# Border by halves, first expert in sequence, last routing in fine steps, no whole float32 weights

## Chip, cores and metric

The kernel runs on one core of one Trainium2 chip. The metric is device microseconds from one launch. A core has a matrix engine (TensorE, PE in the profile; PEld are its weight loads), a vector engine (VectorE, DVE), a scalar engine (ScalarE, ACT), GpSimd (POOL) and SyncE (SP), which here only issues transfers. Each engine works through its own queue in order, and waits at an instruction until what it needs is there. Transfers are issued from SP, ACT and POOL.

## What is computed

Retention attention over two batches (768 steps, 8 heads of 64), then two mixture-of-experts layers (MoE) over the 1536 tokens of width 512, each with 8 experts of inner width 1024. The first skips tokens whose skip score is not positive and adds its result to x; the second places at most a capacity of tokens per expert, in order.

```python
for t in range(S):
    state = gamma * state + k[:, :, t] (outer) v[:, :, t]
    y[:, :, t] = scale * q[:, :, t] @ state
...
do_compute = x @ w_skip > 0                      # first MoE
e_idx = argmax(xc @ w_gate); gate_w = softmax at e_idx
out[do_compute] = xc + gate_w * (relu(xc @ w1[e]) @ w2[e])
...
e = argmax(x @ w_gate2)                          # second MoE
keep token i if fewer than capacity tokens before it chose e
out[i] = gate_w[i] * (relu(x[i] @ w1[e]) @ w2[e])
```

## The kernel before

**Attention.** The 768 steps are cut into six chunks c of 128, and units (c, b) run over chunks and batches. `scores` (L592) forms q k products, which DVE multiplies by a decay mask into p (L607); `state` adds k v products into u (L620), for which POOL scales k with `scale_k` (L575, the tile is called big, since k and v lie in a raw buffer of that name) and q with `scale_q` (L591); `outs` forms the result xt (L637, L644). Beside it a generator `sink` routes the chunk before: logits (L375), their sums (L385), a choice by DVE (mx, d, rm, t, tm, m, then the gate's se, sf and a reciprocal), transposed rows rowc (L394), ranks (L313 ff.), slots (pr, sl, where) and `to_slots` (L327), which adds token numbers into a slot table tab. The rows of a chunk are written to a table in memory by `write_rows` (L339). Between steps, `pump` moves weights one piece on.

**Weights.** Chunks of 1 MB (w1a, w2a of MoE 1, w1b, w2b of MoE 2; two halves j per expert) are loaded by SP into five raw buffers, all called big (L210). A chunk is then divided into two float32r parts, hi by ACT (L237) and lo by DVE (L240, raw minus hi): in the attention in pieces of 128x512, later of 128x1024, so that a chunk is two pieces of each. A product with divided operands is three matmuls (`mm3`, L759 to L761: hi hi, lo hi, hi lo). Four of MoE 1's chunks (w2a of the odd experts, j = 1) are not divided but used as whole float32 (L789), with a whole transposed hTw. In the attention, pump divides on two of three turns from chunk 1 on.

**Border.** `last_chunk` (L461) routes the last chunk one batch after the other and gathers expert 0's rows from the chunks before into a0 (issued in `sink`, L346); `place` (L356) adds the last chunk's rows through a one-hot oh, then a0 through the identity, and `split` (L362, L363) makes xh on ACT and xl on DVE, by which layer 1 of expert 0 begins.

**Experts.** For expert e, `layer1` gives h (24 matmuls of 128x512, called s in the rows), h is transposed into hT (L738) and split into hTh and hTl, the next expert's rows are transposed into x, and `layer2` (24 matmuls, called o) runs one expert behind. Its result goes to `route_b` (L806), a generator stepped beside the main line: DVE makes row (L810, x plus gated result), TensorE transposes it (L824), forms the second MoE's logits (L830, L835), DVE chooses (mx to reciprocal), then ranks and slots (prb, slb, whereb), and `to_slots`. The order of every engine's queue is the order in which this code issues. `step_side` advances the generators and pump.

**Second MoE.** After the last routing, blocks (0,0) and (0,1) of expert 0 (128 rows each) run singly, then experts 1 to 7 in pairs of blocks (256 columns). The rows of a block are gathered by ids_b. `emit_out` (L860) scales a result on ACT into y and scatters it from POOL.

Of the kernel before, what the change touches and what calls it, by code (L numbers as in the profile page):

```python
# [41 lines left out]
def kernel(  # L42
# [53 lines left out]
    def load_first():  # L96

        qk, kv = qk_tile(a_p), take_kv()
        for b in range(B):
            nc.sync.dma_start(out=qk[:, :, b], in_=qkv[0, :, 0:2, b])  # L100
            nc.sync.dma_start(out=kv[:, 1, b], in_=qkv[0, :, 3, b])
        nc.sync.dma_start(out=kv[:, 0], in_=qkv[0, :, 2])
        return qk, kv
# [101 lines left out]
    def load_w():  # L205
        while count["load"] < len(order) and len(raw_free) > kept[0] and raw_free[0][0] <= count["turn"]:
# [4 lines left out]
            key, _, divided = order[i]  # L211
            if divided:
                raw_t[i] = (t, count["turn"])
            else:
                wt[key], held[key] = t.rearrange("p (k f) -> p k f", k=4), t

    def next_split():

        while count["split"] < len(order) and not order[count["split"]][2]:
            count["split"] += 1  # L220
# [24 lines left out]
    def used(key):  # L245
        pool = held.pop(key)
        if key in whole_keys:
            raw_free.append((0, pool))
        else:
            w_free.append((count["turn"] + 2, pool))  # L250

    whole_keys = {o[0] for o in order if not o[2]}
# [29 lines left out]
    def pick(lg, nt, ng, rm, gate_out):  # L282
# [10 lines left out]
        ex = sm.tile([128, n, 8], F32, tag=f"ex{n}", name="ex")  # L293
        nc.scalar.activation(out=ex, in_=d, func=ACTF.Exp)
        t = t9[n]
        nc.vector.scalar_tensor_tensor(out=t[:, :, 0:8], in0=d, scalar=0.0, in1=rm, op0=ALU.is_equal, op1=ALU.mult)
        tm = sm.tile([128, n, 1], F32, tag=f"tm{n}", name="tm")
# [4 lines left out]
        def gate():  # L302
            se = sm.tile([128, nt, ng, 1], F32, tag=f"se{n}", name="se")
            nc.vector.tensor_reduce(out=se, in_=ex.rearrange("p (a g) j -> p a g j", a=nt), axis=AX.X, op=ALU.add)  # L304
            sf = sm.tile([128, nt, ng], F32, tag=f"sf{n}", name="sf")
            nc.vector.tensor_scalar(out=sf, in0=se.rearrange("p a g o -> p a (g o)"), scalar1=1e-9, scalar2=None, op0=ALU.add)
            nc.vector.reciprocal(out=gate_out, in_=sf)
# [925 lines left out]
```

## Time and profile before

| | us |
|---|---|
| median of three runs (414.24 to 416.0) | 414.49 |
| the profiled execution | 413.43 |
| its span in the trace | 411.6 |
| TensorE busy | 381.8 |
| DVE busy | 247.3 |
| ACT busy | 210.0 |
| POOL busy | 119.4 |

The profiled execution took 1.8 us more than its span, and 1.06 less than the median. Times inside the trace count from the span's start. In rows of a timeline the bracket behind an operation gives the idle time of its engine just before it, and what ended it. "x4" merges four like instructions; their time runs from the first's start to the last's end, and since matmuls overlap, distances are best read from one start to the next.

### The profile page before, as it was taken

To read this page: it belongs to the slowest core of one execution; us is meant where nothing else is said; L and a number is where in the kernel's file an instruction comes from. 1 tells how busy PE (TensorE), PEld (TensorE's weight loads), DVE (VectorE), ACT (ScalarE), POOL (GpSimd) and SP (SyncE) were. 2 spreads that over 40 slices of the span, in tenths; PEclk is the share of its full clock that TensorE was granted. 3 is DMA by queue.
4 is the path that set the end of the run, shared out by engine and by line. 5 is a ranking of instruction groups with operands and counts; after the bars stand their busy time and mean duration, and the time that the engine had idled before them with its cause. 6 is when DMAs were issued, how large, how long until landed. Compare 5 with 4: busy or idle time off the path is not lost.

```text
span 411.6 us, 6872 instructions
## 1 busy us (share of the span) xinstructions
PE 381.8 (93%) x2665; PEld 311.9 (76%) x2665; DVE 247.3 (60%) x440; ACT 210.0 (51%) x318; POOL 119.4 (29%) x184
## 2 busy tenths in 40 slices
PE   8879999688999999999886999999999999999993
PEld 4768778566767667766554899898989889898982
DVE  4646776549896896896652497274555637364310
ACT  1435553258776677667431665374535556354301
POOL 3665764271044043033034210311304030130202
PEclk8998999989999999999999999999999999999998
DMA  8997965749988887987963287475865657520101
GB/s 292 418 419 279 352 245 148 304 117 352 388 298 335 325 304 285 344 273 287 344 233 91 83 265 262 161 258 204 271 217 182 216 184 231 191 76 2 50 3 39
DMA packets 18336, 95.99 MB, mean 233 GB/s; under 512 B 2481, under 2 KB 2737, under 8 KB 8824
## 3 DMA queue, kind: packets, MB, share of 16 engines
q1 hardware_dynamic: 12068, 80.33, 53.6%
q0 software_dynamic: 3280, 9.76, 7.3%
q10 hardware_dynamic: 2948, 5.39, 3.5%
q8 instruction: 23, 0.38, 0.4%
q14 instruction: 17, 0.14, 0.1%
HBM read 87.03 MB, written 9.48 MB: 234 GB/s over the span
## 4 chain that ended last, share of the span: by engine, by line
PE 66%; DVE 12%; DMA 10%; ACT 6%; issue 5%; POOL 1%; SPq 0%; POOLq 0%; DVEq 0%; ACTq 0%
PE s L759 10%; PE s L761 10%; PE s L760 10%; PE o L761 7%; PE o L759 7%; PE o L760 7%; DVE lo L240 5%; DMA big<-in_w1a_dram 4%; ACT hi L237 4%; PE o L789 2%; DMA table<-rowc 2%; DVE xl L363 2%; PE m L644 2%; DMA wgt<-in_wg_dram 2%; PE m L637 1%
## 5 line engine op out<-in xcount | busy, mean ns | idle before, releaser
L240 DVE TENSOR_TENSOR lo<-big,hi 128x1024 fp32r<-128x1024 f32 (+1 forms) x126 | 145.1, 1184 | 56.0 <-ACT hi L237 55.4
L237 ACT ACTIVATE hi<-big 128x1024 fp32r<-128x1024 f32 (+1 forms) x126 | 121.8, 1014 | 3.5 <-DMA big<-in_w1a_dram 3.5
L759 PE MATMUL o<-hi,hTh 128*128 128x512 f32 x176 | 72.1, 409 | 0.3 <-ACT hTh L362 0.3
L761 PE MATMUL o<-hi,hTl 128*128 128x512 f32 x176 | 70.0, 398 | 1.0 <-DVE hTl L363 1.0
L760 PE MATMUL o<-lo,hTh 128*128 128x512 f32 x176 | 69.7, 396 | 0.0
L761 PE MATMUL s<-xh,lo 128*128 128x256 f32 x224 | 63.4, 283 | 0.0
L760 PE MATMUL s<-xl,hi 128*128 128x256 f32 x224 | 63.4, 283 | 0.0
L759 PE MATMUL s<-xh,hi 128*128 128x256 f32 x224 | 63.4, 283 | 0.0
L865 POOL DMA_INDIRECT out_dram<-y,ixo x16 | 18.2, 1137 | 142.2 <-ACT y L862 121.8
L759 PEld LDWEIGHTS s<-xh,hi 128*128 128x128 f32 x224 | 43.0, 192 | 0.3
L760 PEld LDWEIGHTS s<-xl,hi 128*128 128x128 f32 x224 | 43.0, 192 | 0.3
L761 PEld LDWEIGHTS s<-xh,lo 128*128 128x128 f32 x224 | 43.0, 192 | 0.0
L761 PEld LDWEIGHTS o<-hi,hTl 128*128 128x128 f32 x176 | 33.1, 188 | 9.7 <-DVE hTl L363 1.8
L759 PEld LDWEIGHTS o<-hi,hTh 128*128 128x128 f32 x176 | 33.1, 188 | 7.1 <-ACT hTh L362 0.5
L760 PEld LDWEIGHTS o<-lo,hTh 128*128 128x128 f32 x176 | 33.3, 189 | 6.7
L996 DVE SCALAR_TENSOR_TENSOR hTl<-s,hTh 128x512 fp32r<-128x512 f32 x28 | 19.3, 688 | 31.7 <-ACT hTh L995 31.7
L759 PE MATMUL s<-hi,xh 128*128 128x512 f32 x80 | 35.5, 444 | 2.2 <-ACT xh L362 1.3
L995 ACT ACTIVATE hTh<-s 128x512 fp32r<-128x512 f32 x28 | 16.7, 598 | 40.2 <-PE s L761 40.2
L862 ACT ACTIVATE y<-o,rowc 128x512 f32<-128x512 f32 x15 | 10.3, 689 | 47.2 <-issue 29.4
L761 PE MATMUL s<-hi,xl 128*128 128x512 f32 x80 | 32.1, 401 | 0.8 <-DVE xl L363 0.8
L760 PE MATMUL s<-lo,xh 128*128 128x512 f32 x80 | 31.9, 399 | 0.0
L842 POOL TENSOR_SCALAR rhsb<-m,cs 128x8 bf16<-128x8 bf16 x8 | 2.5, 306 | 85.2 <-DVE se L304 73.3
(151 smaller groups left out, 545.2 us busy)
## 6 DMA issues: line engine op xcount, KB each, us to landing
big<-in_w1a_dram SPq DMA_DIRECT2D x16, 1024.0 KB, 6.6
big<-in_w2a_dram SPq DMA_DIRECT2D x16, 1024.0 KB, 6.8
big<-in_w1b_dram SPq DMA_DIRECT2D x16, 1024.0 KB, 5.4
big<-in_w2b_dram SPq DMA_DIRECT2D x16, 1024.0 KB, 5.0
qk<-in_qkv_dram SPq DMA_DIRECT2D x5, 1024.0 KB, 9.8
big<-in_qkv_dram SPq DMA_DIRECT2D x5, 1024.0 KB, 6.4
table<-rowc ACTq DMA_DIRECT2D x5, 516.0 KB, 7.7
table<-row ACTq DMA_DIRECT2D x8, 258.0 KB, 4.0
```

The source lines that it names most:

```text
L237: nc.scalar.activation(out=hi[:, k], in_=r3[:, k], func=ACTF.Copy)
L240: nc.vector.tensor_tensor(out=lo[:, k], in0=r3[:, k], in1=hi[:, k].bitcast(F32), op=ALU.subtract)
L363: nc.vector.tensor_tensor(out=lo, in0=src, in1=hi.bitcast(F32), op=ALU.subtract)
L644: nc.tensor.matmul(out=o[64 * j:64 * j + 64, 128 * r:128 * r + 128], lhsT=v[:, b, 2 * r + j, :], rhs=pt[c, b][j][:, r, :], start=not c and ...
L759: nc.tensor.matmul(out=acc, lhsT=a[0], rhs=w[0], start=first, stop=False)
L760: nc.tensor.matmul(out=acc, lhsT=a[0], rhs=w[1], start=False, stop=False)
L761: nc.tensor.matmul(out=acc, lhsT=a[1], rhs=w[0], start=False, stop=last)
L789: nc.tensor.matmul(out=acc, lhsT=a[0][:, k % 4, :], rhs=w[:, k % 4, :], start=k == 0, stop=k == FT - 1)
L862: nc.scalar.activation(out=y, in_=acc, func=ACTF.Copy, scale=xs[:, GCOL + 1:GCOL + 2])
L865: new = nc.gpsimd.indirect_dma_start(out=out[:, :], out_offset=bass.IndirectOffsetOnAxis(ap=ix, axis=0), in_=y, in_offset=None, bounds_che ...
L995: nc.scalar.activation(out=hi[:, g:g + 2, :], in_=acc, func=ACTF.Relu)
L996: nc.vector.scalar_tensor_tensor(out=lo[:, g:g + 2, :], in0=acc, scalar=0.0, in1=hi[:, g:g + 2, :].bitcast(F32), op0=ALU.max, op1=ALU.subtract
```

## The change

It does seven things. (1) The first loads: v of both batches comes in one transfer instead of two, after the qk of both. (2) No weight is used whole: all of w2a is divided. (3) The order of weights has w2a of expert 0 ahead of w1a of expert 1, and the main line runs layer 2 of expert 0 directly after its layer 1; from expert 1 on layer 2 is again one behind. (4) In the attention pump divides on three of four turns from chunk 2 on; `scale_k` and the decays are issued earlier. (5) The rows of a chunk are written before the ranks are formed; the last chunk's rows go out in one transfer from SP; the border places and splits by halves, and slot sums, ids and gathers of the last chunk (`gather_all`) are issued after the first six matmuls of expert 0. (6) `mm3s` takes two k at a time, four matmuls with hi and then two with lo; x of the next expert is turned after the first six matmuls of layer 2, and `to_slots` of an expert comes one step later. (7) The last routing is stepped between matmuls of layer 1 of block (0,0), in fine steps; x of block (0,1) is transposed after all of layer 2, and the last y is scaled half on ACT and half on DVE.

```diff
-        nc.sync.dma_start(out=kv[:, 0], in_=qkv[0, :, 2])
+        for i in (1, 0):
+            nc.sync.dma_start(out=kv[:, i], in_=qkv[0, :, 2 + i])
...
-            order.append(((kind, e, j), ap[e, j], not whole(kind, e, j)))
-
-    def whole(kind, e, j):
-
-        return kind == "w2a" and e % 2 == 1 and j == 1
+            order.append(((kind, e, j), ap[e, j]))
...
-        if e:
-            add_chunks(w2a, e - 1, "w2a")
+        if e != 1:
+            add_chunks(w2a, e - 1 if e else 0, "w2a")
...
             rows_T(xt, rc, 1, psum)
+            write_rows(nc.scalar, rc, B)
             yield
...
             where = [slots_of(sl, i) for i in bs]
-            write_rows(nc.scalar, rc, B)
...
             place(acc, *late[0], True, False)
-            where = [slots_of(sl[b], 0) for b in range(B)]
-            for b in range(B):
-                gates[b]()
-                write_rows(nc.scalar, rc[:, b:b + 1, :], 1)
-            place(acc, *late[1], False, False)
-            for b in range(B):
-                to_slots(where[b], rhs[b][:, 0], 0, 16)
-            nc.vector.tensor_copy(out=ids, in_=tab)
...
+            gate(ex, B, 2, rc[:, :, GCOL:GCOL + 2])
+            write_rows(nc.sync, rc, B)
             for g in range(2):
                 ks = slice(2 * g, 2 * g + 2)
+                place(acc, *late[1], False, False, range(KT)[ks])
                 place(acc, a0, ident, False, True, range(KT)[ks])
...
+            def gather_all():
+                where = [slots_of(sl[b], 0, sm, "whereb", 2) for b in range(B)]
+                for b in range(B):
+                    to_slots(where[b], rhs[b][:, 0], 0, 16)
+                nc.vector.tensor_copy(out=ids, in_=tab)
+                for e in (1, 0, 2, 3):
+                    xs1[e] = gather(ids[:, e:e + 1], 1 + NT)
...
-                pump(4, count["turn"] % 3 > 0)
+                pump(4, c >= 2 and count["turn"] % 4 > 0)
...
+            if b == 0 and 0 < c < NCH - 1:
+                scale_k(c)
             yield
...
-                if c + 1 < NCH - 1:
-                    scale_k(c + 1)
...
+    def mm3s(acc, pairs, first, last):
+
+        todo = [(a[0], w[i]) for a, w in pairs for i in range(2)] + [(a[1], w[0]) for a, w in pairs]
+        for i, (a, w) in enumerate(todo):
+            nc.tensor.matmul(out=acc, lhsT=a, rhs=w, start=first and i == 0, stop=last and i == len(todo) - 1)
+            if i % 2 and i < len(todo) - 1:
+                yield
...
-        yield from idle(2 if e < E - 1 else 1)
+        yield from idle(3 if e < E - 1 else 1)
         to_slots(where, rhs, 8, 8)
...
+    h0 = []
+    first = layer1(x, "w1a", 0, h0)
+    next(first)
+    x0[1]()
+    step_side()
+    h = run(first)
+    xs1[4] = gather(ids[:, 4:5], 1 + NT)
+    second = layer2(h0, "w2a", 0)
...
+        if e > 1:
+            second = layer2(hT.pop(e - 1), "w2a", e - 1)
+            next(second)
+            step_side()
+            x = turned(xs1[e + 1] if e + 1 < E else a0, 0, "x")
...
+            acc = run(second)
+            then_route(e - 1, acc, *((2, 1) if e < E - 1 else (0, 0)))
...
+    last = route_b(E - 1, xs1[E - 1], acc, 0, 0)
+    next(last)
+    pieces[0] = 0
...
+    first = layer1(x, "w1b", 0, h0, True)
+    for i in range(1, 13):
+        next(first)
+        if i % 3 == 0:
+            step_side()
+        if i in (2, 4, 5, 9, 12):
+            next(last)
```

The first place is DVE's queue at the end of chunk 1's routing in the attention, where the first weight split stands (where are the slots, lo the split, p the masked scores, mx to m the choice for the next chunk). Before:

```order
L420 TENSOR_SCALAR where<-iota,sl 128x257 x2
L240 TENSOR_TENSOR lo<-big_88,hi 128x512
L607 TENSOR_TENSOR p<-s,mask 128x512 x2
L240 TENSOR_TENSOR lo<-big_88,hi 128x512
L607 TENSOR_TENSOR p<-s,mask 128x512 x2
L287 TENSOR_REDUCE mx<-s 128x4
```

After, from the same slots on:

```order
L412 TENSOR_SCALAR where<-iota,sl 128x257 x2
L605 TENSOR_TENSOR p<-s,mask 128x512 x4
L272 TENSOR_REDUCE mx<-s 128x4
L275 TENSOR_TENSOR d<-s,mx 128x32
L261 SCALAR_TENSOR_TENSOR rm<-s,cs 128x2x8 x2
```

Two pieces of lo that stood ahead of the two pairs of p have gone behind the choice.

The second place is SP's queue around the border, from the last k and v load on (big from in_w1a or in_w2a are weight chunks, table is the write of the last chunk's rows). Before, where that write is on ACT's queue:

```order
L82 DMA big_89<-in_qkv_dram 128x2048
L210 DMA big_85<-in_w2a_dram 128x2048
L210 DMA big_88<-in_w2a_dram 128x2048
L210 DMA big_86<-in_w1a_dram 128x2048
L210 DMA big_89<-in_w1a_dram 128x2048
L210 DMA big_87<-in_w2a_dram 128x2048
```

After:

```order
L82 DMA big_88<-in_qkv_dram 128x2048
L206 DMA big_85<-in_w2a_dram 128x2048
L206 DMA big_89<-in_w1a_dram 128x2048
L206 DMA big_86<-in_w1a_dram 128x2048
L328 DMA table<-rowc_108 128x2x516
L206 DMA big_87<-in_w1a_dram 128x2048
L206 DMA big_88<-in_w1a_dram 128x2048
```

The two loads of expert 2's w1a now stand behind the table write of the last chunk; before, they followed the loads ahead of them without a write between.

The third place is DVE's queue in the last routing, around the row of expert 7 (row with the second number; the first line closes the gate of expert 6, or follows it). Before:

```order
L307 RECIPROCAL row_1188<-sf 128x1
L240 TENSOR_TENSOR lo<-big_88,hi 128x1024 x2
L810 SCALAR_TENSOR_TENSOR row_1189<-o,rowc_107 128x512
L848 TENSOR_TENSOR prb<-t,m 128x8
L850 TENSOR_REDUCE slb<-prb 128x1
L852 TENSOR_SCALAR whereb<-iota,slb 128x257
L287 TENSOR_REDUCE mx<-t 128x1
```

After:

```order
L298 RECIPROCAL row_1153<-sf 128x1
L230 TENSOR_TENSOR lo<-big_86,hi 128x1024
L850 TENSOR_TENSOR prb<-t,m 128x8
L852 TENSOR_REDUCE slb<-prb 128x1
L854 TENSOR_SCALAR whereb<-iota,slb 128x257
L230 TENSOR_TENSOR lo<-big_86,hi 128x1024
L811 SCALAR_TENSOR_TENSOR row_1154<-o,rowc_106 128x512
L272 TENSOR_REDUCE mx<-t 128x1
```

The slots of expert 6 (prb, slb, whereb), which wait for its ranks, now stand ahead of expert 7's row, between the two lo pieces.

## Rows read from the trace of the kernel before

**Rows 1.** Stretches: PE, PEld, DVE, ACT, POOL busy, granted PE clock, DMA share, GB/s.

```profile
32.00:35.40 3.40, 3.40 (x41) 3.28 (x38) 2.66 (x13) 2.37 (x7) 1.78 (x3) 0.51 1.01 419
222.00:226.00 4.00, 1.40 (x9) 1.14 (x9) 0.00 (x0) 0.59 (x1) 3.08 (x4) 1.00 0.54 148
120.00:210.00 90.00, 85.22 (x447) 60.16 (x447) 70.33 (x125) 56.60 (x84) 22.43 (x37) 1.00 0.84 305
226.00:390.00 164.00, 164.00 (x1051) 147.85 (x1050) 91.43 (x106) 85.42 (x113) 32.20 (x41) 1.00 0.52 179
```

**Rows 2.** Whom PE waits for, whole span: us in total, times, longest.

```profile
PE t L738 <- DMA rowc<-table,ids_b: 2.6, 1, 2.6
...
PE s L375 <- DVE p L607: 2.0, 1, 2.0
PE t L824 <- DVE row L810: 1.9, 2, 1.5
...
PE u L620 <- POOL big L575: 1.3, 2, 1.0
...
PE t L738 <- ACT h L779: 1.1, 1, 1.1
PE o L761 <- DVE hTl L363: 1.0, 1, 1.0
```

**Rows 3.** Timeline, DVE then ACT, before 30: start, us, operation, idle before it.

```profile
28.38 0.89 DVE L240 TENSOR_TENSOR lo<-big,hi 128x512 fp32r<-128x512 f32 x1 [4.50 <-ACT hi L237]
...
27.72 1.15 ACT L237 ACTIVATE hi<-big 128x512 fp32r<-128x512 f32 x2 [3.23 <-DMA big<-in_w1a_dram]
```

**Rows 4.** The chain that ended last, at the border: start, us, what.

```profile
69.35 6.62 DMA table<-rowc
...
76.83 4.47 DMA a<-table,ids
...
83.43 0.79 PE s L759
```

**Rows 5.** Transfers issued at 56 to 68, then 69.2 to 80: KB, us to landing.

```profile
table<-rowc ACTq DMA_DIRECT2D x1, 516.0 KB, 4.3
...
big<-in_w1a_dram SPq DMA_DIRECT2D x2, 1024.0 KB, 6.0
```

**Rows 6.** Timeline of DVE at the border and in the experts of MoE 1.

```profile
82.51 0.87 DVE L363 TENSOR_TENSOR xl<-m,xh 128x256 fp32r<-128x256 f32 x2 [2.77 <-ACT xh L362]
...
89.55 2.36 DVE L240 TENSOR_TENSOR lo<-big,hi 128x1024 fp32r<-128x1024 f32 x2 [4.36 <-ACT hi L237]
...
127.98 0.17 DVE L287 TENSOR_REDUCE mx<-t 128x1 f32<-128x8 f32 x1 [3.08 <-PE t L835]
...
142.97 0.17 DVE L287 TENSOR_REDUCE mx<-t 128x1 f32<-128x8 f32 x1 [1.37 <-PE t L835]
...
153.00 0.74 DVE L810 SCALAR_TENSOR_TENSOR row<-o,rowc 128x512 f32<-128x512 f32 x1
...
158.05 0.17 DVE L287 TENSOR_REDUCE mx<-t 128x1 f32<-128x8 f32 x1 [3.11 <-PE t L835]
...
188.09 0.17 DVE L287 TENSOR_REDUCE mx<-t 128x1 f32<-128x8 f32 x1 [3.09 <-PE t L835]
```

**Rows 7.** Timeline of PE around one expert of MoE 1.

```profile
147.66 1.88 PE L789 MATMUL o<-big,hTw 128*128 128x512 f32 x4
149.74 0.26 PE L327 MATMUL tab<-rhsb,whereb 128*128 128x8 bf16 x4 [0.20 <-DVE whereb L852]
...
152.45 0.48 PE L759 MATMUL s<-hi,xh 128*128 128x512 f32 x1
...
153.93 0.60 PE L824 MATMUL t<-cs,row 128*128 128x128 f32 x4
```

**Rows 8.** Timeline of PE, the first matmul of block (0,1).

```profile
226.69 0.47 PE L759 MATMUL s<-hi,xh 128*128 128x512 f32 x1
```

**Rows 9.** Timeline of ACT, the last result.

```profile
404.77 0.69 ACT L862 ACTIVATE y<-o,rowc 128x512 f32<-128x512 f32 x1 [2.12 <-PE o L761]
```

More of the change, by code (lines that the diff above doesn't have):

```diff
@@ L210, in load_w @@
             nc.sync.dma_start(out=t, in_=order[i][1])
[L211 to L215, printed above, removed]
+            raw_t[i] = (t, count["turn"])
     def next_split():
-        while count["split"] < len(order) and not order[count["split"]][2]:
-            count["split"] += 1
         i = count["split"]
@@ L245, in used @@
     def used(key):
[L246 to L252, printed above, removed]
+        w_free.append((count["turn"] + 2, held.pop(key)))
     splitting = []
@@ L677, in main @@
                 yield from scores(c, 1)
+                if c and c + 1 < NCH:
+                    decays(c + 1)
                 if c == 0 and pump:
@@ L784, in layer2 @@
         acc = psum("o", 2)
-        for k in range(FT):
+        for k in range(0, FT, 2):
             w = wt[kind, e, k // 4]
             a = hT[k // 4]
-            if whole(kind, e, k // 4):
-                nc.tensor.matmul(out=acc, lhsT=a[0][:, k % 4, :], rhs=w[:, k % 4, :], start=k == 0, stop=k == FT - 1)
-            else:
-                mm3(acc, at_k(a, k % 4), at_k(w, k % 4), k == 0, k == FT - 1)
-            if k % 4 == 3 and done_with(kind, e):
+            ks = (k % 4, k % 4 + 1)
+            for _ in mm3s(acc, [(at_k(a, i), at_k(w, i)) for i in ks], k == 0, k == FT - 2):
+                pass
+            if k % 4 == 2 and done_with(kind, e):
                 used((kind, e, k // 4))
-            if k % 2 == 1:
-                yield
+            yield
         return acc
@@ L919, in then_route @@
         return g
-    for e in range(E):
-        h = run(layer1(x, "w1a", e))
+    h0 = []
[7 more added lines that the diff above has]
+    next(second)
+    h0.append(turned(h, 1, "hT"))
+    step_side()
+    next(second)
+    step_side()
+    x = turned(xs1[1], 0, "x")
+    acc = run(second)
+    then_route(0, acc, 1, 1)
+    for e in range(1, E):
+        first = layer1(x, "w1a", e)
+        if e == 1:
+            for _ in range(2):
+                next(first)
+                step_side()
+            x = turned(xs1[2], 0, "x")
+        h = run(first)
         if e + 4 < E:
@@ L941, in load_block @@
         xs2[e, j] = gather(ids_b[:, 8 * j + e:8 * j + e + 1])
-    def after_routing():
-        while last in side:
-            yield
-        nc.vector.tensor_copy(out=ids_b, in_=tab[:, 8:24])
-        for e, j in ((0, 1), (1, 0), (1, 1), (2, 0), (2, 1)):
-            load_block(e, j)
-        yield
-    side.append(after_routing())
-    h0 = []
-    h = run(layer1(x, "w1b", 0, h0))
+    h0 = []
+    first = layer1(x, "w1b", 0, h0, True)
+    for i in range(1, 13):
+        next(first)
+        if i % 3 == 0:
+            step_side()
+        if i in (2, 4, 5, 9, 12):
+            next(last)
+    try:
+        next(first)
+    except StopIteration as stop:
+        h = stop.value
+    nc.vector.tensor_copy(out=ids_b, in_=tab[:, 8:24])
+    for e, j in ((0, 1), (1, 0), (1, 1), (2, 0), (2, 1)):
+        load_block(e, j)
+    second = layer2(h0, "w2b", 0)
+    next(second)
     h0.append(turned(h, 1, "hT"))
-    second = layer2(h0, "w2b", 0)
-    for _ in range(FT // 2 - 1):
-        next(second)
-        step_side()
+    acc = run(second)
     while side:
@@ L961 @@
     x = turned(xs2[0, 1], 0, "x")
-    acc = run(second)
+    pieces[0] = 1
     ct = totals([cum[:, 0, :], cumb])
@@ L1021 @@
     h = run(layer1(x, "w1b", 0, h0))
+    second = layer2(h0, "w2b", 0)
+    next(second)
+    h0.append(turned(h, 1, "hT"))
+    step_side()
     x = pair_T(1)
-    h0.append(turned(h, 1, "hT"))
     flag = overflow(ct)
-    acc = run(layer2(h0, "w2b", 0))
+    acc = run(second)
     emit_out(xs2[0, 1], acc)
```

163 lines of the change are left out of this document (87 added, 76 removed).

## Prediction, made before the change was run

> **What bounds the kernel now.** I read the table of stretches first [rows 1]. From 226 to 390, which is the pair loop of the second MoE, TensorE works in all 164.00 of 164 us: nothing there can be gained by an order. From 120 to 210, the experts of the first MoE, it works 85.22 of 90, and the rest of its idle time lies in the attention, at the border between attention and MoE, and at the last routing. So the second view is who TensorE waits for [rows 2]: 1.3 us for POOL's scaled k, 2.0 for the product with the mask (p), 2.6 for a gather, 1.9 for row, 1.1 for h, 1.0 for hTl. Behind each I looked at the releaser's engine. The p that came late stood on DVE behind a weight split lo, which had waited 4.50 us for ACT's hi, which had waited 3.23 us for a weight load from memory [rows 3]. At the border the chain is a write of the table (6.62 us), then the gather that reads it (4.47 us), and the first expert matmul starts at 83.43 [rows 4].
>
> In the experts I ask which engine sets the period. Per expert DVE runs from mx (142.97) through six lo pieces, an xl and the slot sums to row (153.00): 10.03 us, and row takes 0.74 [rows 6]. TensorE transposes that row (153.93), and 4.12 us later the next mx can start (158.05) [rows 6, 7]. A closed loop DVE to TensorE to DVE of 10.03 + 0.74 + 0.05 + 4.12 = 14.9 us. From mx at 127.98 to mx at 188.09 there are four periods of 15.03 [rows 6]. So DVE's queue is nearly the bound already, though it works fewer of the 90 us than TensorE does.
>
> **The attention: -5.0 us.** Splits now begin with chunk 2, not 1, so the first lo is queued behind the where and p of chunk 1 and finds its weights landed: the 2.0 (1.97) goes. POOL scales k before the gate work and the decays: the 1.3 goes. Behind the late p the clock fell to half: 0.51 granted over 3.4 us, so 3.4 x 0.49 = 1.7 us [rows 1]. If the idle goes, I count that too. Sum 5.0. The same twelve split pieces lie in later turns, between masks and gate work that leave DVE gaps, and the earlier scaling only changes the order on POOL, before operations that wait for TensorE anyway. Bounds: 3.3 if the half-clock stretch comes anyway, 5.3 if the start's two combined v loads also hide the 0.3 us wait for qk.
>
> **The border: -2.2 us.** An equal write of 516 KB with nothing beside it landed in 4.3 us; this one took 6.62 because two 1 MB loads were issued with it [rows 5]. In the new order no weight load stands on SP between expert 1's first-layer chunks and the last chunk's table write, so chunk 4's write should land at about 73.5 and its gather at 78 to 79 instead of 81.3. TensorE gets there at about 77.5. By halves (two transposes, a 128x256 split of 0.43, then matmuls) I work out the first expert matmul at 81.2 instead of 83.43. The slot sums leave this path and stand behind the first six matmuls. Bounds: 0 if the write is no faster, 2.7 if the gather hides wholly. The last chunk's write goes from two on ACT to one on SP, where the next loads queue behind it; they have six chunks of work ahead of them.
>
> The Trainium skill (DMA: Bandwidth & Descriptors, section Issuing engines are not separate DMA queues) says that transfers issued by different engines run on the same 16 DMA engines and interleave. By that rule the move of a write from ACT to SP is worth nothing in itself, and any load still landing at 69 slows the write as the two loads do now: with one in flight the border's term would be about 1.1, not 2.2. By the rows the last load ahead of it should have landed by then, so I keep 2.2, and the smaller value belongs to the second rival.
>
> **No whole weights: TensorE less, DVE more.** Two k of a whole weight take 1.88 us (from 147.66 to 149.74, less the 0.20 wait before it); in the divided form the six matmuls of two k take 1.48 from start to the next operation (152.45 to 153.93), some 1.41 of it their own [rows 7]. That frees 0.47 twice per odd expert, 0.93, and 3.7 in all on TensorE. In exchange four more chunks are split: 8 lo pieces of about 1.16 = 9.3 us of DVE and four hTl. TensorE's saving is on the path only where TensorE sets the pace, and by the loop above it does not.
>
> **Experts 0 to 5: -2.5 us.** From xl (82.51) to the end of the second row (127.98 less 4.2) lie 41.2 us, in which DVE idles 7.5 in seven gaps: 33.7 us of work. The new order has the same work there (22 lo pieces in both; expert 0's second layer comes earlier, but the queue to row 1 is as long), plus 1.0 for slot sums moved behind xl. It starts 2.2 earlier, at 80.3, and keeps the longest gap, 4.36 [rows 6], because ACT's next hi still stands behind h. So row 1 ends at about 119.5 (TensorE cannot be there before 118.4: 21 sixes of 1.48, small work, and 1.7 for half clock), and mx 1 follows at 123.7 instead of 127.98: 2.1 beyond the border. Then four periods of 14.92 for 15.03: 0.4. The expert loop gains almost nothing, since DVE holds the same six lo between mx and row; TensorE's freed time turns into a wait of about 0.8 before each row's transposes. Bounds: 0.9 lost if all seven gaps of this stretch return, 6.8 gained if TensorE paces (first rival).
>
> **The last routing: -2.8 us.** From mx 5 (188.09) to the second block (226.69) before takes 38.6 [rows 6, 8]. The waits for row (1.5 of 1.9), h, hTl and the gather, 6.2 [rows 2], two short ones (0.8) and the last whole step (0.9) go: the routing is threaded through layer 1 of the block, and the gather lies under 18 matmuls. New waits: row 6 stands behind one more lo (about 1.6), row 7 behind lo, slots and another lo (about 3.0), 0.4 for the last slots and 0.6 for x, which is now turned after all of layer 2. 38.6 - 7.9 + 5.6 = 36.3; the finer order lets 0.5 of the new waits overlap: 35.8. Bounds: 7.4 gained with no row wait, 0.6 lost if half clock follows both long ones.
>
> **Second MoE and tail: -0.3 us.** The pairs have the same matmuls, and DVE works 91 of 164 us there: 0. The last y took 0.69 on ACT [rows 9]; halves on ACT and DVE take about 0.43, as the 128x256 xl does [rows 6].
>
> Sum: 5.0 + 2.2 + 2.5 + 2.8 + 0.3 = 12.8, off a profiled execution of 413.43: 400.6. The median shown stands 1.06 above that execution, so 401.7 is the forecast, 3.1% faster.
>
> **The rivals.** First: TensorE paces the experts. If the later lo pieces fit elsewhere, the period falls to TensorE's own work, 15.0 less its waits of 0.7 and 0.2, 14.1; with its floor of 118.4 at row 1 the experts give 6.8 instead of 2.5: 397.4. For it: three quarters of DVE's time are busy, not all. Against it: six lo still stand between mx and row. Second: attention or border gain fails, because the write meets the tail of an earlier load (2.2) or the half-clock stretch comes at another place (1.7): 403.9 to 405.6. A late gather for expert 1 belongs here: it is issued 1 us later than now and has about 4 us before its transposes. Third: the 9.3 us of added lo reach the path, each expert's row later by 1.3: 411.0. For it: ACT's hi stands behind h, and lo behind hi. Against it: two lo fit into the 4.12 us after each row.
>
> Fourth, slower: TensorE now waits before nearly every row transpose, seven times about 0.8 and twice 1.6 to 3.0. After the 1.97 wait the clock fell to half for 3.4 us; if each of nine waits did that, 9 x 1.7 = 15.3 would turn -12.8 into +2.5: 417.0. It decides from nine stretches on. Against it: waits of 0.2 to 0.5 between 120 and 210 left the granted clock at 1.00, and so did the 2.6 between 222 and 226 [rows 1].
>
> The Trainium skill (TensorE: Matmul & The Clock Gate, section HAM oscillation) describes a kernel whose clock was throttled again at each repeated wait; by that rule this rival would hold. The trace shows both, a fall after 1.97 and none after 2.6, so it keeps a small chance.
>
> **How the numbers follow.** Forecast 0.55, TensorE-paced 0.10, lost attention or border gain 0.20, lo on the path 0.09, half clock 0.06. The range takes in the first three (0.85), with the bounds of the border and experts: 396.5 to 407.5. Under 0.5% (2.1 us) a measurement of this kernel can't tell a change from none. Faster by more: 0.55 + 0.10 + 0.20 and half of the 0.09, 0.89; within: 0.05; slower: 0.06.
>
> **What would show it.** Attention: no wait for p near 30 and no half clock at 32 to 35; the wait for big at the state's matmuls gone. Border: the table write near 4.3 us and the first expert matmul about 7 us earlier than 83.43 (5.0 + 2.2). Experts: a period of 14.9, with TensorE waiting 0.7 to 0.8 for row before the transposes and no wait for whereb; a period of 14.1 would prove the first rival, over 15.5 the third, and a granted clock below 1.00 between 110 and 210 the fourth. Last routing: no gather wait, but 1.6 and 3.0 for the last two rows. I am wrong if the period moves by more than 0.5, since that counts seven times.

## The result, and the profile after

The changed kernel takes 405.5 us (median of four, 405.26 to 405.78); the kernel before, measured beside it, 415.25. The ratio is 0.9765 [0.9733, 0.9796], so it is 2.3% faster. Forecast were 401.7 and 3.1%: the sign and the range held, the size did not. The profiled execution of after takes 405.45 with a span of 403.7, 7.9 below the 411.6 of before. The page of after, its first lines and the costliest group:

```profile
span 403.7 us, 6932 instructions
PE 377.1 (93%) x2680; PEld 314.4 (78%) x2680; DVE 254.4 (63%) x449; ACT 218.5 (54%) x327; POOL 119.9 (30%) x184
...
L230 DVE TENSOR_TENSOR lo<-big,hi 128x1024 fp32r<-128x1024 f32 (+1 forms) x134 | 155.0, 1183 | 52.8 <-ACT hi L227 51.9
```

TensorE is 4.7 us less busy than before (381.8), DVE 7.1 us more (247.3): the change has moved work from the engine that is busiest to the one whose queue sets the pace of the experts. To see where the 7.9 lie, I cut both spans at the same instructions and took differences of their start times.

| stretch, from one mark to the next | before | after | difference | forecast |
|---|---|---|---|---|
| start to chunk 0's logits | 14.39 | 16.30 | +1.91 | 0 |
| to chunk 4's logits | 50.06 | 43.02 | -7.04 | -5.0 |
| to the first expert matmul | 18.98 | 15.63 | -3.35 | -2.2 |
| to mx 1 (mx of expert 1) | 44.55 | 42.90 | -1.65 | -2.1 |
| to mx 5, four periods | 60.11 | 59.93 | -0.18 | -0.4 |
| to block (0,1) | 38.60 | 41.01 | **+2.41** | **-2.8** |
| to the last matmul | 177.60 | 177.29 | -0.31 | 0 |
| to the end | 7.31 | 7.62 | +0.31 | -0.3 |

From chunk 0's logits to the first expert matmul everything came as forecast or better. The last routing, where 2.8 were to be gained, lost 2.4. That is the error of 5.2, larger than the whole miss of 3.8 between the two medians.

Whom TensorE waits for in after (us in total, times, longest), to be held against [rows 2]:

```profile
PE t L825 <- DVE row L811: 11.4, 8, 4.5
...
PE s L760 <- DVE xl L352: 0.9, 1, 0.9
```

The waits for p, scaled k, the gather, h and hTl of [rows 2] are gone or under 0.5. In their place stand eight waits for row, 11.4 in all. The timeline of after, in order of time (start, us, operation, idle before it; ACTq is a transfer issued from ACT's queue), first the border, then the experts with the mark mx, then the last routing from row 6 (the row of expert 6) on, then the tail:

```profile
63.83 0.37 ACTq L328 DMA_DIRECT2D table<-rowc  x1
...
68.48 1.24 POOL L335 DMA_INDIRECT a<-table,ids  x1 [3.37 <-DVE m L288]
...
74.95 0.50 PE L760 MATMUL s<-hi,xh 128*128 128x512 f32 x1 [0.93 <-DVE xl L352]
...
117.85 0.17 DVE L272 TENSOR_REDUCE mx<-t 128x1 f32<-128x8 f32 x1 [0.77 <-PE t L836]
...
132.83 0.17 DVE L272 TENSOR_REDUCE mx<-t 128x1 f32<-128x8 f32 x1 [0.73 <-PE t L836]
...
177.78 0.17 DVE L272 TENSOR_REDUCE mx<-t 128x1 f32<-128x8 f32 x1 [0.78 <-PE t L836]
...
189.88 0.63 PE L825 MATMUL t<-cs,row 128*128 128x128 f32 x4 [2.04 <-DVE row L811]
...
196.06 0.16 DVE L298 RECIPROCAL row<-sf 128x1 f32<-128x1 f32 x1
...
196.31 0.33 ACTq L328 DMA_DIRECT2D table<-row  x1
196.68 2.00 ACT L227 ACTIVATE hi<-big 128x1024 fp32r<-128x1024 f32 x2 [1.35 <-POOL rhsb L845]
...
197.77 1.23 DVE L230 TENSOR_TENSOR lo<-big,hi 128x1024 fp32r<-128x1024 f32 x1 [1.55 <-ACT hi L227]
...
199.57 1.22 DVE L230 TENSOR_TENSOR lo<-big,hi 128x1024 fp32r<-128x1024 f32 x1
200.70 0.74 DVE L811 SCALAR_TENSOR_TENSOR row<-o,rowc 128x512 f32<-128x512 f32 x1
...
201.59 1.09 PE L825 MATMUL t<-cs,row 128*128 128x128 f32 x4 [4.53 <-DVE row L811]
...
218.79 0.50 PE L760 MATMUL s<-hi,xh 128*128 128x512 f32 x1 [0.66 <-ACT xh L351]
...
396.57 0.47 ACT L865 ACTIVATE y<-o,rowc 128x256 f32<-128x256 f32 x1 [2.12 <-PEq L1187]
...
397.07 0.48 DVE L867 TENSOR_SCALAR y<-o,rowc 128x256 f32<-128x256 f32 x1 [10.47 <-ACT y L865]
```

At the border the gather is issued 4.65 us after the table write (68.48 less 63.83), where before 7.48 lay between (76.83 less 69.35, [rows 4]), and TensorE no longer waits for it. The experts' period is 14.98 (59.93 over four), as the loop of DVE said.

The last routing shows the failure instruction by instruction. The table write of expert 6's row (L328), which the change issues earlier, stands on ACT's queue and needs the gate's reciprocal, which ends at 196.22. The hi pieces of the next weights stand behind that write and begin at 196.68. DVE's lo needs hi and waits 1.55. The slots stand behind this lo, another lo behind the slots, and row of expert 7 behind that. TensorE, which wants this row, idles 4.53. Then the clock. Stretches of after (PE, PEld, DVE, ACT, POOL busy, granted PE clock, DMA share, GB/s):

```profile
201.50:203.50 2.00, 1.91 (x7) 1.75 (x8) 0.00 (x0) 0.60 (x1) 0.00 (x0) 0.50 0.83 217
203.50:205.50 2.00, 2.00 (x13) 0.87 (x12) 0.00 (x0) 0.28 (x1) 0.00 (x0) 0.50 0.76 315
205.50:207.50 2.00, 2.00 (x10) 1.68 (x9) 1.03 (x7) 0.21 (x1) 0.00 (x0) 0.91 0.00 0
...
120.00:190.00 70.00, 64.76 (x367) 49.40 (x366) 63.62 (x105) 51.27 (x72) 16.01 (x30) 1.00 0.88 309
...
190.00:192.00 2.00, 2.00 (x18) 1.44 (x17) 0.00 (x0) 1.40 (x2) 0.00 (x0) 1.00 0.91 254
```

After the long wait TensorE works for some four microseconds at 0.50, the 1.2 GHz level, which costs by my estimate 2 x 0.50 + 2 x 0.50 + 2 x 0.09 = 2.2 us. Between 120 and 190, with waits of 0.8 before each of rows 2 to 5, the granted clock is 1.00, and so it is behind the wait of 2.04 before row 6 (190 to 192).

### The profile page after: what moved, and what is told of

The parts are those of the page before. It is cut to its first block, busy times and chain, and to the rows that moved or that the text cites. A ratio compares the mean times of both kernels' runs of the same rounds, so it can differ in the third digit from the quotient of the medians.

```text
span 403.7 us, 6932 instructions
## 1 busy us (share of the span) xinstructions
PE 377.1 (93%) x2680; PEld 314.4 (78%) x2680; DVE 254.4 (63%) x449; ACT 218.5 (54%) x327; POOL 119.9 (30%) x184
## 5 line engine op out<-in xcount | busy, mean ns | idle before, releaser
L230 DVE TENSOR_TENSOR lo<-big,hi 128x1024 fp32r<-128x1024 f32 (+1 forms) x134 | 155.0, 1183 | 52.8 <-ACT hi L227 51.9
L227 ACT ACTIVATE hi<-big 128x1024 fp32r<-128x1024 f32 (+1 forms) x134 | 130.9, 1016 | 2.6 <-POOL rhsb L845 1.3
L752 PE MATMUL o<-hi,hTh 128*128 128x512 f32 x112 | 44.9, 401 | 0.0
L753 PE MATMUL o<-lo,hTh 128*128 128x512 f32 x112 | 44.4, 396 | 0.0
L865 ACT ACTIVATE y<-o,rowc 128x512 f32<-128x512 f32 (+1 forms) x15 | 10.1, 675 | 46.7 <-issue 29.4
L760 PE MATMUL o<-hi,hTh 128*128 128x512 f32 x80 | 33.1, 414 | 0.0
L760 PE MATMUL o<-lo,hTh 128*128 128x512 f32 x80 | 31.7, 396 | 0.0
L760 PE MATMUL s<-hi,xl 128*128 128x512 f32 x80 | 25.6, 402 | 0.0
```

What stands on the lines that cost most here:

```text
L227: nc.scalar.activation(out=hi[:, k], in_=r3[:, k], func=ACTF.Copy)
L230: nc.vector.tensor_tensor(out=lo[:, k], in0=r3[:, k], in1=hi[:, k].bitcast(F32), op=ALU.subtract)
L752: nc.tensor.matmul(out=acc, lhsT=a[0], rhs=w[0], start=first, stop=False)
L753: nc.tensor.matmul(out=acc, lhsT=a[0], rhs=w[1], start=False, stop=False)
L760: nc.tensor.matmul(out=acc, lhsT=a, rhs=w, start=first and i == 0, stop=last and i == len(todo) - 1)
L865: nc.scalar.activation(out=y[:, 0:n], in_=acc[:, 0:n], func=ACTF.Copy, scale=xs[:, GCOL + 1:GCOL + 2])
```

## Experiments

The first five below are on the last routing and the experts' loop. My theory: in the last routing row 7 is late because hi, lo and slots stand ahead of it on their queues, and the lost clock follows from that wait; in the experts DVE's loop sets the period, so that row, not TensorE's work, must come earlier. The rivals: the wait is made by something else that is late (the matmuls before row, a load), and TensorE's own work sets the period.

**e1, the table write of expert 6's row late again.** The write goes behind the slots, as for the earlier experts.

```diff
-        if e >= E - 2:
+        if e >= E - 1:
...
-        if e < E - 2:
+        if e < E - 1:
```

> The changed kernel, with one thing undone: the table write of expert 6's row is issued on ACT after the slots, as before the change, so that one hi piece stands ahead of it. DVE's order is the same. Order theory: in the changed kernel ACT stands 1.35 us at that write, which waits for the gate's reciprocal; hi is behind it, lo waits 1.55 us for hi, and row 7 is behind lo. Then the first lo starts about 1.4 earlier, row 7 at about 199.3 instead of 200.70, TensorE waits about 3.1 instead of 4.5, and the time falls by 1.4 to about 404.1. Rival, that lo itself and the slots' chain fill the time: row 7 stays within 0.3 of 200.7 and the time at 405.5.

It takes 403.06 (0.9748 [0.9713, 0.9783]). The timeline of TensorE:

```profile
198.45 1.08 PE L825 MATMUL t<-cs,row 128*128 128x128 f32 x4 [3.08 <-DVE row L811]
```

The wait for row 7 falls from 4.53 to 3.08, which is the size I had forecast for it, and the stretch from mx 5 to block (0,1) from 41.01 to 38.95. So the write on ACT's queue made 1.45 of that wait; with a little less half clock the stretch gains 2.06. The whole time is 2.4 below that of after, but the four executions of e1 alone lie 2.6 apart, so the gain is read from the stretch. The rest of the wait is mostly the two lo, as e4 shows.

**e4, the two lo behind row 7.** `pieces` (how many weight pieces a side step may divide) is held at zero from the third step of expert 7's layer 2 on and let go for two steps of the next layer 1, so that slots and row 7 come first.

```diff
+        pieces[0] = int(i < 2)
...
-    pieces[0] = 0
...
+            pieces[0] = int(i < 9)
...
+            pieces[0] = 0
```

> The changed kernel, with the two weight pieces that stand ahead of expert 7's row on ACT and DVE moved behind it (no piece in the last two steps of expert 7's second layer, two in the first steps of the next layer 1). Order theory: row 7 starts as soon as the slots of expert 6 are through, near 197.0 instead of 200.70; TensorE waits under 1 us before its transposes instead of 4.5, the clock stays at 1.00 there, and the time falls by 3.6 (wait) plus about 2.2 (half clock), to about 399.9. Rival, that the clock falls anyway: about 401.9. Rival, that the moved pieces come too late for the second half of the block's layer 2 or delay expert 7's routing: a wait for lo or for slots of 1 to 3 us there, 402 to 404.

It takes 401.26 (0.9682 [0.9646, 0.9718]). TensorE's timeline, and the stretch behind row 7:

```profile
197.81 0.63 PE L825 MATMUL t<-cs,row 128*128 128x128 f32 x4 [0.62 <-DVE row L811]
...
207.04 0.26 PE L316 MATMUL tab<-rhsb,whereb 128*128 128x8 bf16 x4 [1.22 <-DVE whereb L854]
```

```profile
198.00:202.00 4.00, 4.00 (x26) 2.76 (x25) 1.74 (x5) 1.92 (x4) 0.00 (x0) 1.00 0.52 185
```

The wait is 0.62, the clock stays at 1.00, and the stretch takes 214.56 - 177.92 = 36.64: 4.4 less than in after, and 2.0 less than before. Part of it returns as a wait of 1.22 for the last slots, behind the lo that were put off. This settles the failed step: the new order of the routing does gain about 2 us, and what took it back were the pieces of weight between expert 6's choice and row 7, and the clock that fell behind them.

**e5, row one step earlier.** For experts 1 to 6 the main line runs layer 2 further before that side step, so that one split piece less stands between mx and row.

```diff
+            for i in range(3 if e < E - 1 else 1):
+                if i:
+                    step_side()
+                next(second)
...
-            then_route(e - 1, acc, *((2, 1) if e < E - 1 else (0, 0)))
+            then_route(e - 1, acc, *((3, 1) if e < E - 1 else (1, 0)))
+            step_side()
```

> The changed kernel, with row issued one split piece earlier on DVE for experts 1 to 6 (one lo that stood ahead of row stands behind it; the same work on every engine). Theory that DVE's queue closes the loop of an expert: from mx to row five lo instead of six, 1.15 less, but then three lo and two hTl after row, 0.5 more than the 4.1 us that TensorE needs to the next mx: the period falls from 14.97 to about 14.4, TensorE's wait before the row transposes from 0.8 to 0.2 or less, and the time by 5 x 0.6 = 3.0 to about 402.5. Rival, that TensorE or ACT sets the period: 14.97 stays and the time too.

It takes 399.33 (0.9639 [0.961, 0.9668]). DVE's timeline, and TensorE's waits:

```profile
117.20 0.15 DVE L272 TENSOR_REDUCE mx<-t 128x1 f32<-128x8 f32 x1
...
131.37 0.15 DVE L272 TENSOR_REDUCE mx<-t 128x1 f32<-128x8 f32 x1
...
173.72 0.16 DVE L272 TENSOR_REDUCE mx<-t 128x1 f32<-128x8 f32 x1
```

```profile
PE t L825 <- DVE row L811: 6.2, 4, 4.5
```

```profile
117.20:173.72 56.52, 56.51 (x321) 43.32 (x320) 53.94 (x94) 44.37 (x64) 13.84 (x26) 1.00 0.95 331
```

The period is 14.13 (56.52 over four), where after has 14.98 (59.93). The same work is done in another order. TensorE's four waits of 0.8 are gone and mx no longer waits for TensorE, which is busy in 56.51 of the 56.52 us. What is left is nearly TensorE's own work, which the first rival of the prediction had at 14.1; DVE, busy for 53.94, is not far behind. In after DVE's loop was the bound, and TensorE's saving from the divided weights was not to be seen for that reason.

**e6, whole weights back** (w2a of the odd experts, j = 1, used whole; all else as in after).

```diff
+        return kind == "w2a" and e % 2 == 1 and j == 1
...
+            if whole(kind, e, k // 4):
+                for i in ks:
+                    nc.tensor.matmul(out=acc, lhsT=a[0][:, i, :], rhs=w[:, i, :], start=False, stop=k == FT - 2 and i == ks[1])
```

> The changed kernel with the second half of w2a of the odd experts used as whole float32 again, all else as changed. Theory of the prediction (DVE's loop sets the period, six lo stand between mx and row either way): TensorE needs 14.1 + 0.9 = 15.1 for an odd expert against a DVE loop of 14.97, so odd experts take 15.1 and the time rises by 0.1 to 0.5. Rival, that TensorE sets the pace: 0.93 for each of four experts, 3.7 more. Rival, that the split work saved (8 lo, 9.3 us of DVE) is on the path: up to 4 us less.

It takes 403.95 (0.978 [0.9729, 0.9831]), and after, run again on the same chip (c_changed), 405.45 (0.9811 [0.9775, 0.9847]): no difference that can be told. Its period is 14.99 (59.97 over four); the way to mx 1 is 1.3 longer and the last routing 1.1 shorter. TensorE's transposes of rows 3 and 5 show where its added work goes:

```profile
143.25 0.66 PE L849 MATMUL t<-cs,row 128*128 128x128 f32 x4 [0.20 <-DVE row L835]
...
173.22 0.66 PE L849 MATMUL t<-cs,row 128*128 128x128 f32 x4 [0.17 <-DVE row L835]
```

In after TensorE waits 0.82 and 0.78 there. The whole form takes 0.6 more of TensorE's time per odd expert, and it comes out of the wait for row. Dividing all weights is worth nothing here, as the prediction said.

> The changed kernel as it is, beside the three below on one chip, since the start of the profile (constants landing at 5.8 to 6.8 us, and a half-clock stretch behind it) came out differently from execution to execution in the runs before these. Theory that the start varies in every kernel and not with the load order: executions of this kernel too fall into two groups about 2 us apart, with granted clocks of about 0.98 and 0.99. Rival, that the changed load order always has the long stretch: all executions near 405.5 and 0.979.

**e10, whole weights once TensorE sets the pace.** The same edit on the best version (e8, below).

> The kernel above with the second half of w2a of the odd experts whole again. In the changed kernel itself whole weights cost nothing, since DVE's loop of 14.97 covered TensorE's 15.06. With row one piece earlier TensorE paces at 14.13, and the whole form should show: odd experts 14.13 + 0.93 = 15.06, even ones 14.13, and the last layer 2 another 0.9: 3 to 4 us more than the kernel above. Rival, that the split work saved on DVE (9.3 us) gives something back: less than 1 more.

It takes 395.81 (0.9561 [0.9496, 0.9626]) against 394.59 for e8 on the same chip, with overlapping runs. DVE's timeline:

```profile
116.44 0.17 DVE L288 TENSOR_REDUCE mx<-t 128x1 f32<-128x8 f32 x1 [1.86 <-PE t L860]
...
130.42 0.17 DVE L288 TENSOR_REDUCE mx<-t 128x1 f32<-128x8 f32 x1 [0.32 <-PE t L860]
...
145.01 0.17 DVE L288 TENSOR_REDUCE mx<-t 128x1 f32<-128x8 f32 x1 [2.60 <-PE t L860]
```

I expected 3 to 4 us of loss and missed. One period in two is 14.59, 0.47 longer than the 14.12 of e8 (56.48 over four), not 0.93, and the other is 13.98, 0.14 shorter. Over four periods the loss is 0.66 (57.14 less 56.48). TensorE's rows give the price of the whole half:

```profile
135.05 3.60 PE L814 MATMUL o<-big,hTw 128*128 128x512 f32 x8
138.48 0.24 PE L332 MATMUL tab<-rhsb,whereb 128*128 128x8 bf16 x4
```

From start to start it takes 3.43, where the divided half takes 2.81 in e8 (137.10 to 139.91). The difference of 0.62 is that of the two periods here (14.59 less 13.98). The 0.14 of the other periods fits DVE's lighter queue: in e8 TensorE starts to transpose a row 0.06 us after DVE has finished it (141.65 + 0.74, then 142.45), while here DVE waits for TensorE before each mx. So where TensorE paces, dividing saves 0.62 per odd expert, and about half of that goes back to the split work on DVE. No run shows this second part by itself.

**e3, the decays late** as before, and only that. They are a product of 128x512 on POOL (gqc).

```diff
-                if c and c + 1 < NCH:
-                    decays(c + 1)
...
+            elif c + 1 < NCH:
+                decays(c + 1)
```

> The changed kernel with POOL's decays (gqc, 1.03 us each) issued after the slot counts again, as before the change; nothing else moves. Theory: in the kernel before, DVE's where (128x257) took up to 1.14 us in place of 0.35 while POOL worked on gqc, and TensorE's slot sums waited 0.68 three times for it. Put back, where takes about 1 us again for chunks 1 to 3 and the time rises by three times 0.7, 2.0. Rival, that the splits' turns made the difference: where stays at 0.35 and the time too.

It takes 407.39 (0.9863 [0.982, 0.9906]), 1.9 more than c_changed, and the way from chunk 0's logits to the first expert matmul is 61.12 against 58.68 there. The timeline of e3, DVE and POOL, and whom TensorE waits for; behind it the same pair of where in c_changed:

```profile
34.39 1.41 DVE L412 TENSOR_SCALAR where<-iota,sl 128x257 bf16<-128x257 f32 x2
...
34.47 1.17 POOL L582 TENSOR_TENSOR gqc<-cs 128x512 f32<-128x512 f32 x1
```

```profile
PE tab L316 <- DVE where L412: 2.2, 4, 0.7
```

```profile
33.73 0.62 DVE L412 TENSOR_SCALAR where<-iota,sl 128x257 bf16<-128x257 f32 x2
```

Three pairs of where that run beside gqc take 1.40 to 1.41 each; with gqc out of the way a pair takes 0.62. TensorE needs where for its next slot sums and waits up to 0.7 for it, 2.2 in all, as the kernel before did (2.0, three times). That accounts for the 2.0 us of the attention that the prediction had not counted: an edit that I had booked as a mere change of POOL's order took a neighbour away from DVE.

**e11, the attention's part alone**, put into the kernel before.

```diff
-                pump(4, count["turn"] % 3 > 0)
+                pump(4, c >= 2 and count["turn"] % 4 > 0)
...
+            if b == 0 and 0 < c < NCH - 1:
+                scale_k(c)
...
+                if c and c + 1 < NCH:
+                    decays(c + 1)
...
-            elif c + 1 < NCH:
-                decays(c + 1)
...
-                if c + 1 < NCH - 1:
-                    scale_k(c + 1)
```

> The kernel before, with the attention's part of the change alone: splits from chunk 2 on, three of four turns, and the earlier scaling of k and earlier decays. By the trace of the changed kernel its stretch from the first to the fifth chunk's logits is 7.0 us shorter: 1.97 (p behind lo), 1.7 (half clock behind that), 1.3 (scaled k), 2.0 (slots slowed while POOL works on the decays). If the attention's part does this alone, the time falls by about 7 to 407; the prediction's working without the slots would give 5.0. Rival, that the moved loads and splits cost the border or the experts something: 2 to 5 less than before in all.

It takes 406.14 (0.9815 [0.9755, 0.9875]) against 415.06, some 7.7 to 8.9 less by ratio and medians. From chunk 0's to chunk 4's logits it needs 43.48, 6.6 less than before, and 1.3 less at the border. So this small part alone makes most of what the whole change gives.

**e9, the border's loads behind the write**, put into the kernel before: the last rows are written from SP, and the two loads of expert 2's w1a follow them.

```diff
-                write_rows(nc.scalar, rc[:, b:b + 1, :], 1)
+                write_rows(nc.sync, rc[:, b:b + 1, :], 1)
...
-                    kept[0] = c < NCH - 1
+                    kept[0] = 1
...
+    kept[0] = 0
```

> The kernel before, with one part of the change: the last chunk's table writes go out on SP, and the two loads of expert 2's first layer stand behind them in SP's queue, so that nothing is loaded beside chunk 4's table write. Theory of the border term: that write lands in about 4.0 us instead of 6.62, the gather behind it 2.6 earlier, TensorE's wait of 1.82 for it goes, and the first expert matmul comes about 1.8 earlier; if the idle before it falls, the half-clock stretch behind it may go too (1.7). In all 1.8 to 3.5 less than before. Rival, that the write is slow for another reason: 6.6 us and no change. Rival, that the later loads delay expert 1's or 2's splits: the gain is given back within the experts.

It takes 411.6 (0.9936 [0.9897, 0.9976]). From chunk 4's logits to the first expert matmul it needs 78.97 - 62.65 = 16.32 instead of 18.98, and the half clock behind the border is gone. Chunk 4's write, its KB and us to landing, then a new wait in TensorE's timeline, and the stretch behind that:

```profile
table<-rowc ACTq DMA_DIRECT2D x1, 516.0 KB, 2.8
```

```profile
87.11 0.69 PE L739 MATMUL t<-cs,rowc 128*128 128x128 f32 x4 [1.97 <-DMA rowc<-table,ids]
```

```profile
88.00:92.00 4.00, 4.00 (x14) 3.07 (x13) 3.57 (x5) 3.76 (x5) 3.22 (x7) 0.62 0.99 347
```

The theory of the border held: without two loads beside it the write lands in 2.8 us, not 6.62 [rows 4], and no one waits for the gather. The loads now lie beside expert 1's gather, and the wait and the half clock come there instead, so that the way to mx 1 is 44.53 as before (44.55). In after expert 0's layer 2 runs next, which does not need that gather, and the wait is not there; no run takes that step back alone.

**e2, first loads as before**, and **e7, two tiles for x of expert 0** instead of a common one.

```diff
-        for i in (1, 0):
-            nc.sync.dma_start(out=kv[:, i], in_=qkv[0, :, 2 + i])
+            nc.sync.dma_start(out=kv[:, 1, b], in_=qkv[0, :, 3, b])
+        nc.sync.dma_start(out=kv[:, 0], in_=qkv[0, :, 2])
```

> The changed kernel with the first loads of the kernel before (v of each batch behind its qk, three transfers for k and v). Theory: in the changed kernel the constants for the masks, queued behind the same bytes, land later and DVE's masks start at 6.79 instead of 5.78; TensorE idles 1.1 us after 7.2 at a clock already falling, and the half-clock stretch lasts to 14.6 instead of 11.4. Undone, the masks start near 5.8, the clock rises near 11.4, the first logits come at about 14.4 instead of 16.3, and all later work moves 1.9 earlier: about 403.6. Rival, that only the wait goes and the clock's stretch stays as long: about 1.0, 404.5. Rival, that chance of the load order between runs made it: no change.

```diff
-            hi = x_p.tile([128, KT, 128], F32R, tag="xh", name="xh")
-            lo = x_p.tile([128, KT, 128], F32R, tag="xl", name="xl")
+            halves = []
...
+                hi = x_p.tile([128, 2, 128], F32R, tag=f"x0h{g}", name="xh", bufs=1)
+                lo = x_p.tile([128, 2, 128], F32R, tag=f"x0l{g}", name="xl", bufs=1)
```

> The changed kernel with the halves of x0 at the border in two tiles each for hi and lo instead of one. In the changed kernel the first expert matmul uses the first half only, which is split by 74.0, but starts at 74.95, right after the second half's lo. Theory that the common tile makes it wait for both halves: with two tiles it starts about 0.9 earlier, near 74.0 less the start's shift, and the time falls by up to 0.9. Rival, that something else ended last (a weight piece or ACT): the wait of 0.93 stays.

Both fell. e2 takes 405.06 (0.978 [0.9747, 0.9812]); its chunk 0's logits start at 15.72, and the half clock between 8 and 15 us is there as in after. So the load order is not shown to cost the 1.91 us that after lost at the start: executions of one and the same kernel differ there. This is c_changed between 8 and 11 us, and then the profiled execution of after:

```profile
8.00:11.00 3.00, 3.00 (x32) 2.88 (x30) 2.26 (x7) 0.42 (x1) 2.06 (x3) 1.00 1.06 393
```

```profile
8.00:11.00 3.00, 2.67 (x16) 2.26 (x16) 2.36 (x7) 0.42 (x1) 2.07 (x3) 0.50 1.05 386
```

With the clock at 1.00 the logits start at 14.91, at 0.50 at 16.30. With the load order of before they start between 14.39 and 15.72 (before, e9, e11, e2), with that of after between 14.58 and 16.62 (e1 and e8 at the ends), so that the order has a small share in it is not excluded. e7 takes 405.17 (0.9788 [0.9748, 0.9828]), and the wait of 0.93 for xl before the first expert matmul is still there, so the common tile does not make it. What does stays open.

**e8, the better version.** Row one step earlier (e5), the lo behind row 7 (e4), and the last y on ACT alone.

```diff
-                    emit_out(xs2[e, j], acc[j], e == E - 1 and j > 0)
+                    emit_out(xs2[e, j], acc[j])
```

> The changed kernel with three edits together: row one piece earlier for experts 1 to 6, the two pieces ahead of expert 7's row moved behind it, and the last y scaled by ACT alone again. If the two gains lie in different places they add up: 399.3 (row earlier) less 4.4 (the last routing's stage with the pieces moved) less 0.3 (in the changed kernel the second half of y, on DVE, started only when ACT's half was done, 0.98 us for both against 0.70 whole): about 394.6. Rival, that with the pieces moved the next wait of the last routing (slots 1.2, h 0.9) grows, since row 6 now comes earlier: 396 to 397.

It takes 394.59 (394.38 to 397.08), 0.9533 [0.9478, 0.9588] of the kernel before, where 394.6 were expected. Whom TensorE waits for:

```profile
PE t L825 <- DVE row L811: 2.3, 4, 1.2
...
PE tab L316 <- DVE whereb L854: 1.2, 1, 1.2
PE m L345 <- DMA a<-table,ids: 1.0, 1, 1.0
```

Of 11.4 us of waiting for row 2.3 are left. The stretch from mx 1 to mx 5 takes 56.48, from mx 5 to block (0,1) 35.51, what the prediction had wanted of the change (35.8). From the last matmul to the end it needs 7.3 instead of 7.62. The wait of 1.0 for the gather, which after does not have, is back in this execution: the load issued at 59.02 took 9.0 us to land (7.5 in after), beside chunk 4's write, and the gather was issued 6.18 us after that write (70.33 less 64.15). The kernel beats both others even so.

## Why the prediction was right and wrong

**The attention: right in kind, larger.** The wait for p, its half clock and the wait for scaled k (2.0 + 1.7 + 1.3) went as forecast. The further 2.0 are the waits for where, three in before, that e3 brought back by one edit.

**The border: right, larger.** The write no longer meets two loads (e9), and in after the gather is hidden wholly, the bound of 2.7 rather than the 2.2 taken. The attention's edit alone gives 1.3 here (e11), so the two overlap. One premise was wrong: the last load ahead of the write had not landed. Issued at 58.70, it took 7.5 us, and so ran beside the write of 63.83:

```profile
big<-in_w1a_dram SPq DMA_DIRECT2D x1, 1024.0 KB, 7.5
```

In after that cost TensorE nothing; in the execution of e8, where the same load landed later, the wait of 1.0 came back. So the gain depends on when that load ends.

**No whole weights, and the period: right, with one price too high.** e6 shows no gain from the first, and e5 that DVE's loop held the period at 14.98, against 14.92 forecast. TensorE waits 0.8 before each of rows 2 to 5, as said. The 0.93 per odd expert set the whole form's time from start to end (1.88) against the divided form's without its end (1.41); from start to start it is 0.62 (e10).

**Experts 0 and 1: 1.65 for 2.1.** The prediction kept the half clock behind the border (0.57 over 83 to 87 in before) as part of TensorE's floor. It went with the gather's wait (1.00 over 75 to 79 in after), yet its 1.7 us did not come on top, which speaks against TensorE as the bound of this stretch. That DVE's queue paces it is what e5 speaks for, where bringing row forward shortens it by 0.84 (to 42.06).

**The last routing: the step that failed.** The wait for row 7, put at "about 3.0", was 4.53, and row 6's, put at 1.6, was 2.04. I had counted the lo and slots that DVE's order shows ahead of row 7, but not ACT's queue behind it: the moved table write waits there for the reciprocal, and hi, and by it lo, stand behind the write (e1: 1.45 of the wait). The second miss is the clock, which the sum put at nothing and only a bound allowed for: "0.6 lost if half clock follows both long ones". The fall behind row 7 alone cost 2.2 by the estimate above, and the stretch lost 2.4. The two rows (1.5 and 0.4 more than forecast), the clock (2.2), two waits that the sum does not have (0.4 for h, 0.3 for m) and the 0.5 of overlap that did not happen make 5.3, against the 5.2 by which this term was off.

**The tail: wrong sign.** The halves of y do not run beside each other: DVE's begins at 397.07, ACT's ends at 397.04. Two halves in a row take 0.98, where one whole takes 0.69 [rows 9]. Both write the same tile y; that the shared tile puts them in sequence is argued, not tried.

**The start.** The forecast had 0 here, and the profiled executions differ by 1.91. That c_changed, the same kernel, starts 1.4 earlier shows that most of it lies in the execution; it is no part of what the prediction reasoned about.

**The rivals.** The lost border, lo on the path and TensorE-paced experts did not happen. The half clock of the fourth came once in after, behind the 4.53, and not nine times. The prediction said that by the Trainium skill this rival would hold; that reads the page too widely. The kernel that the Trainium skill describes (TensorE: Matmul & The Clock Gate, section HAM oscillation) is throttled again at each repeated wait, but its waits are longer, by that page's figures, than those before rows 0 to 6 here. These, of 0.2 to 2.04, left 1.00 in after; the 4.53 in after and, in e1, the 3.08 did not, and in e7 the 2.03 before row 6 did not either (last section).

## What to carry to other kernels

When an issue of a transfer is moved onto a compute engine's queue, list what stands behind it there and who waits for that in turn: a write that costs 0.33 us on ACT made TensorE wait 1.45 longer, two engines away. Before work is taken off the busiest engine, find whether another engine's queue closes the loop; here an order that brought one instruction forward on DVE (e5) gave 0.85 us per expert, and the saved matmuls gave nothing without it. A long wait can cost more than its length: behind the one of 4.53 the clock fell, at some 2.2 us more.

## What was not expected of the hardware

A where of 128x257 on DVE takes 0.35 us alone and, in before, up to 1.14 while POOL multiplies a tile of 128x512; POOL's product takes 1.17 beside it and 1.04 otherwise. The length of a wait alone does not tell whether the clock falls: it fell after 1.97 in before [rows 1, 2] and after 1.97 in e9, and not after 2.6 in before. Before row 6 TensorE waits 2.04 in after, and the clock stays at 1.00; in e7 it waits as long there, and the clock falls:

```profile
188.79 0.63 PE L829 MATMUL t<-cs,row 128*128 128x128 f32 x4 [2.03 <-DVE row L815]
```

```profile
190.00:194.00 4.00, 4.00 (x18) 2.49 (x17) 2.09 (x2) 2.28 (x4) 0.00 (x0) 0.57 0.51 213
```

What tells the two apart is not shown. At the start, too, the clock falls in one execution of the changed kernel and not in another, and the logits come 1.4 us later with it.
